# Attention with a sink and a window, then an MLP: where the sink scores of two pairs of chunks are computed

## The chip, the cores and the metric

The kernel runs on one core of a Trainium2 chip. The metric is the device time of one execution in microseconds. A second number is the span: the time from the first to the last instruction in the profile of one execution. TensorE (PE) does the matrix products, VectorE (DVE) and ScalarE (ACT) the work on elements, GpSimd (POOL) small work and the issue of loads, SyncE (SP) the issue of stores and of transposes by DMA.

## The reference

Attention for 4 batches, 8 heads, 768 positions of 64 elements; a query sees the first 4 positions (the sink) and the 128 positions up to its own. The result is reshaped to rows of 512, normalised, put through a two-layer MLP and added to itself.

```python
scores = scale * np.matmul(q, k.transpose(0, 1, 3, 2))
is_sink = pos[None, :] < int(n_sink)               # n_sink = 4
rel = pos[:, None] - pos[None, :]
in_window = (rel >= 0) & (rel < int(window))       # window = 128
scores = np.where(is_sink | in_window, scores, -1000000000.0)
a = softmax(scores);  x = (a @ v) as rows of 512   # shortened
xn = (x - mu) / np.sqrt(var + 1e-06) * g_ln
out = x + np.maximum(xn @ w_ch1, 0.0) @ w_ch2
```

## The kernel before

The 3072 rows are 24 tiles of 128 rows (index t), two to a chunk (index c, 0 to 11), three chunks to a batch. So chunks 3, 6 and 9 begin a batch, chunks 5, 8 and 11 end one.

Every operation is written down once with `P.op(name, engines and costs, priority, emit, reads, writes, ...)`. `Plan.run` (line 114) then plays the program through with the costs, picks on each engine the ready operation of the lowest priority number, and gives out buffers from rings. The order it arrives at is emitted. So what a change of a priority or of a cost does to the order is seen only in the order itself. Rings that matter here: `nat` (8 buffers, line 415) for queries and keys as loaded, `kT` (4) and `qT` (3, line 419) for the transposed ones, `ps` (3, line 421) for the sink weights, and the PSUM banks `one` (4) and `pair` (2).

From chunk 4 on, `chunk(c)` (line 654) issues for k and q two loads each on POOL (line 704; 128 KB each, four to a chunk), and on SP two transposes by DMA for each (`DMA_TRANSPOSE`, issued in `dma_t`, line 578). The loads wait for `gate(c)`: the small step `rs` (lines 891 and 892, on POOL) of an earlier tile. The transposes of q also wait for the transpose of a normalised tile (`trx`, also line 578, xnt<-xc in the profile), which the matrix stage L1047 of that chunk reads. Loads of v follow (`load_m`, line 632).

From chunk 3 on, `block(t)` (line 916) is one visit of TensorE for a tile. It has four parts in this order: the products of the tile before with v (L954, L961, L970), the scores of tile t inside the window (L981, `pair` banks, pieces of 64 by 64), and in a chunk's first visit the sink scores of both its tiles (L989): eight matmuls that give 32 rows each to a strip of the output and are 128 columns wide (64 in a batch's first chunk). ACT makes exponentials of the scores (L999) and of the sink scores (L1009, into `ps`). Between the visits run the MLP's products: `mlp(c)` (line 1029) with L1047 (the first layer, reads xnt) and L1075 (the second).

The last loop (from line 1093 on) calls `chunk(c)` and `block` in order of c.

Of the kernel before, what the change touches and what calls it, by code (L numbers as in the profile page):

```python
# [9 lines left out]
AF = mybir.ActivationFunctionType  # L10
# [215 lines left out]

LOW, HIGH = 1e-9, 1e9
LAST_CUTS, LAST_ACT = (0, 320, 512), (3,)
NEG = -1e30
NEVER = -1e9  # L230
BIG = 3.3e38
# [138 lines left out]
def kernel(  # L370
# [203 lines left out]
    def gate(c):  # L574
        return [rs_op[2 * c - (4 if c > 5 else 5)]] if PAR["by_dma"] < c < NC else []
# [78 lines left out]
    def chunk(c):  # L654
        b, R = c // RC, c % RC
        d = at(c, "tr") if c >= 2 else early(2 * c)
        ld = d - 14.0 if c >= RC else 4.0
        if c < 2:
            kT_b[c], qT_b[c] = Buf(f"kT{c}", "kT"), Buf(f"qT{c}", "qT")
            if c == 0:  # L660
                nats = [Buf("kf", "natf"), Buf("qf", "natf")]
                for hh in range(2):
                    hs = slice(4 * hh, 4 * hh + 4)
                    for i, (x, T) in enumerate(((k, kT_b[c]), (q, qT_b[c]))):
                        nm, src, part = "kq"[i], nats[i], Buf(f"{'kq'[i]}l{hh}")
                        ap = x[b, hs, 0:256, :].rearrange("h (p i) d -> p h (i d)", i=2)
                        P.op(f"{nm}ld{hh}", {("SP" if i == 0 else "ACT"): (0.53, 0.53)}, -70 + hh,
                             lambda e, src=src, ap=ap, hs=hs: (nc.sync if e == "SP" else nc.scalar).dma_start(
                                 src.t[:, hs].rearrange("p h i d -> p h (i d)"), ap), writes=[src, part], dma=HW_F)
                        nat, pt, done = Buf(f"{nm}c{hh}", "natc"), Buf(f"pt{nm}{hh}", "one"), Buf(f"{nm}T0{hh}")  # L670
                        P.op(f"cast{nm}{hh}", {"DVE": dve(512), "ACT": act(512)}, d + 0.01 * hh,
                             lambda e, nat=nat, src=src, hs=hs: (nc.scalar.copy if e == "ACT" else V.tensor_copy)(
                                 nat.t, src.t[:, hs].rearrange("p h i d -> p i h d")),
                             reads=[part], hold=[src], writes=[nat])

                        def tr(e, pt=pt, nat=nat):
                            pb = pt.t.rearrange("p (h i m) -> p h i m", h=2, i=2)
                            for hp in range(2):
                                for i in range(2):
                                    nc.tensor.matmul(pb[:, hp, i, :], lhsT=nat.t[:, i, 2 * hp:2 * hp + 2, :], rhs=ident,  # L680
                                                     start=hp + i == 0, stop=True, skip_group_check=True)
                        o = P.op(f"tr{nm}{hh}", pe(0.23), d + 0.02 + 0.01 * hh, tr, reads=[nat, Bc["ident"]], hold=[T], writes=[pt])
                        trs[0], trs[1] = trs.get(0, [o]), [o]
                        evict(f"ev{nm}0{hh}", d + 0.05 + 0.01 * hh, 512,
                              lambda pt=pt: pt.t.rearrange("p (h i m) -> p h m i", h=2, i=2),
                              lambda T=T, hh=hh: T.t[:, 2 * hh:2 * hh + 2, :].rearrange("p h (m i) -> p h m i", i=2), [pt], [T, done], fp=True)
                        for t in range(2):
                            tile_of[nm, t, hh] = done
            else:
                for i, (x, T) in enumerate(((k, kT_b[c]), (q, qT_b[c]))):  # L690
                    by_pairs(c, [("kq"[i], x, T, PAR["ld1"] + 0.01 * i)], d + 0.01 * i)
        else:
            both = []
            for nm, src, bT in (("k", k, kT_b), ("q", q, qT_b)):
                T = Buf(f"{nm}T{c}", nm + "T")
                bT[c] = T
                if c < PAR["by_dma"]:
                    both.append((nm, src, T, ld + (0.1 if nm == "q" else 0.0)))
                    continue
                for i in range(2):  # L700
                    nat = Buf(f"{nm}n{c}{i}", "nat")
                    ap = src[b, :, 256 * R + 128 * i:256 * R + 128 * (i + 1), :].rearrange("h p d -> p h d")
                    P.op(f"{nm}ld{c}{i}", {"POOL": (0.87, 0.9)}, ld + 0.01 * i + (0.1 if nm == "q" else 0.0),
                         lambda e, nat=nat, ap=ap: G.dma_start(nat.t, ap), writes=[nat], dma=SW, after=gate(c))  # L704
# [211 lines left out]
    def block(t):  # L916
# [4 lines left out]
        if t < NT:  # L921
# [11 lines left out]
            reads += [kT, qT] + ([kprev] if r and not i else []) + ([kts_b[b]] if sinks else [])  # L933
            writes += pps + ([pp_s] if sinks else [])
            hold += pes + ([held["ps", c]] if sinks else [])
# [14 lines left out]
        def go(e):  # L950
# [24 lines left out]
            for hp in range(HP):  # L975
                u, col = hp // 2, 192 * (hp % 2)
                for g, kt, k0, c0, q0, n in ((u, kT, own, 0, own, 128), *([(1 - u, kprev, old + 64, 0, own, 128)] if r else []),
                                             *([(u, kprev, old, 128, own, 64)] if r else []), (1 - u, kT, own + 64, 128, own + 64, 64)):
                    for h2 in range(2):
# [1 line left out]
                        nc.tensor.matmul(pps[u].t[64 * g:64 * g + 64, h2, col + c0:col + c0 + n],  # L981
                                         lhsT=kt.t[rs, hp, k0:k0 + 64], rhs=qT.t[rs, hp, q0:q0 + n],
                                         start=col == 0 and c0 == (128 if g != u and not r else 0), stop=True, skip_group_check=True)
            if sinks:
                for hp in range(HP):
                    for qh in range(2):
                        u = hp // 2
                        p0 = 64 * (qh ^ u) + 32 * (hp % 2)
                        nc.tensor.matmul(pp_s.t[p0:p0 + 32, 128 * u + 64 * (not r):128 * u + 128], lhsT=kts_b[b].t[:, hp, :],  # L989
                                         rhs=qT.t[:, hp, :].rearrange("p (i u c) -> p u i c", i=2, u=2)[:, qh, 0 if r else 1:2],  # L990
                                         start=True, stop=True, skip_group_check=True)
        cost = (0.0 if t == NT else 0.33 if r else 0.22) + (0.0 if not last else (0.36 if lr else 0.24) + (0.12 if lr else 0.06) + (0.115 if last["ps"] else 0.0))
        end = t < NT and sinks
        P.op(f"sc{t}", pe(cost + ((0.2 if r else 0.15) if end else 0)), d, go, reads=reads, writes=writes, hold=hold, mode=(("n" if lr else "r") if last else "q", "c" if end else "q"))
        if t < NT:
            scores.setdefault(c, P.ops[-1])
            for j in range(n_pair):
# [9 lines left out]
            if sinks:  # L1007
                lo = 0 if r else 64
                P.op(f"sx{c}", {"ACT": act(256 - 2 * lo)}, d + 0.3, lambda e: nc.scalar.activation(  # L1009
                    held["ps", c].t.rearrange("p (u c) -> p u c", u=2)[:, :, lo:128],  # L1010
                    pp_s.t[:, 0:256].rearrange("p (u c) -> p u c", u=2)[:, :, lo:128], AF.Exp, scale=scale),
                     reads=[pp_s], writes=[held["ps", c]])
        if last:
            st, x, xc = last["made"]
            x_b[t - 1], xst_b[t - 1] = x, st
# [191 lines left out]
```

## Time and profile before

| what | value |
| --- | --- |
| median of 3 runs | 215.82 us (215.72 to 217.69) |
| the profiled execution's own time | 215.85 us |
| its span | 214.3 us |
| L1047 and L1075 on TensorE | 86.5 and 84.3 us busy |
| L989 on TensorE, all sink scores | 72 matmuls; 48 of 128 columns, 24 of 64 |
| the first and the last of them start | 47.7 and 174.3 us |
| queue of POOL's loads (q0) | 13.18 MB |
| queue of SP's and ACT's transfers (q1) | 13.71 MB |

PE is the engine's matmuls, PEld its weight loads, SPq the DMA instructions that SP issues. A row of a timeline has the start and the length in microseconds (from the first start to the last end of the merged instructions), the engine, the line, the operation, output<-input, the tile in rows*columns, the shape, and the count. "(idle before <-releaser)" is in brackets where the engine stood idle. A few per cent of the matmul records are missing from a trace.

### The profile page before, as it was taken

The numbers are of one execution on the slowest core, as the hardware profiler recorded it, in microseconds if no ns is written. First come the engines' busy times: TensorE is split into PE (matmuls) and PEld (weight loads), VectorE is DVE, ScalarE is ACT, GpSimd is POOL, SyncE is SP. The second block draws the span as 40 slices with busy tenths as digits, with TensorE's granted clock in tenths as the row PEclk, the third lists the DMA queues.
The fourth block names the chain that finished last, engine by engine and source line by source line (L and its number), as shares of the span: only waits on it lengthen the run. The fifth ranks groups of instructions, "written<-read, shape, count | busy, mean of one in ns | idle before, by whom it ended". The sixth has DMA issues, their size and how long they took to land.

```text
span 214.3 us, 6540 instructions
## 1 busy us (share of the span) xinstructions
PE 205.8 (96%) x2682; PEld 143.4 (67%) x2704; DVE 114.3 (53%) x316; ACT 110.2 (51%) x179; POOL 112.4 (52%) x167
## 2 busy tenths in 40 slices
PE   7799999999999999999999999999999999999994
PEld 2567874755865865864865865864865865865853
DVE  4688884798355356356355456446355445444021
ACT  3797488195652562562562562562562562530610
POOL 7978732499971980970970980971971201202000
PEclk9999999999999999999999999999999999999999
DMA  5999999999999999899799999799899302202103
GB/s 152 189 189 206 193 208 192 177 162 161 159 192 152 135 139 125 129 132 175 105 147 133 98 145 161 120 129 162 111 137 137 98 3 73 77 0 74 52 0 107
DMA packets 104586, 28.04 MB, mean 131 GB/s; under 512 B 94820, under 2 KB 101608, under 8 KB 104552
## 3 DMA queue, kind: packets, MB, share of 16 engines
q0 software_dynamic: 69904, 13.18, 86.1%
q1 hardware_dynamic: 33448, 13.71, 35.8%
q10 hardware_dynamic: 1200, 0.69, 1.1%
q8 instruction: 22, 0.36, 0.8%
q14 instruction: 12, 0.10, 0.2%
HBM read 27.43 MB, written 6.29 MB: 157 GB/s over the span
## 4 chain that ended last, share of the span: by engine, by line
PE 92%; DMA 3%; DVE 1%; issue 1%; ACT 1%; ACTq 0%; DVEq 0%
PE one L1047 39%; PE one L1075 39%; PE pair L981 3%; DMA natf<-in_q_dram 3%; PE one L954 2%; PE one L961 2%; PE one L970 1%; PE one L989 1%; PE pair L731 1%; PE one L859 1%; PE one L899 1%; PE pair L606 1%; PE one L599 1%; PE pair L752 0%; PE pair L859 0%
## 5 line engine op out<-in xcount | busy, mean ns | idle before, releaser
L1075 PE MATMUL one<-w,h 128*128 128x512 bf16 (+2 forms) x378 | 84.3, 370 | 2.2 <-issue 1.6
L1047 PE MATMUL one<-xnt,w 128*128 128x256 bf16 x768 | 86.5, 273 | 0.0
L1047 PEld LDWEIGHTS <-w 128*128 128x128 bf16 x768 | 74.8, 98 | 11.2 <-issue 0.4
L1057 ACT ACTIVATE h<-one 128x512 bf16<-128x512 f32 x95 | 56.7, 597 | 47.3 <-PE one L1047 47.3
L1075 PEld LDWEIGHTS <-h 128*128 128x128 bf16 x400 | 37.1, 98 | 40.1
L999 ACT ACTIVATE pe<-pair 128x768 bf16<-128x768 f32 x36 | 27.2, 809 | 41.0 <-PE pair L981 41.0
L891 POOL TENSOR_SCALAR st<-st 128x1 f32<-128x1 f32 x24 | 9.0, 373 | 66.7 <-DVE st L884 66.2
L646 POOL DMA_DIRECT2D vn<-in_v_dram x59 | 38.7, 704 | 9.2 <-DMA w<-in_moe_w_ch_dram 6.7
L1022 DVE RECIPROCAL rec<-one 128x4 f32<-128x4 f32 x36 | 6.4, 178 | 63.0 <-PE one L970 51.5
L1084 DVE SCALAR_TENSOR_TENSOR ot<-one,st,x 128x512 f32<-128x512 f32 (+2 forms) x25 | 18.2, 727 | 20.3 <-PE one L1075 14.2
L892 POOL TENSOR_TENSOR st<-st,mhalf 128x1 f32<-128x1 f32 x24 | 16.8, 701 | 2.0
L882 DVE BATCH_NORM_STATS2 st<-x 128x6 f32<-128x512 bf16 x24 | 16.7, 695 | 0.8
L1024 DVE TENSOR_TENSOR x<-one,rec 128x256 bf16<-128x256 f32 x36 | 15.3, 425 | 1.2
L704 POOL DMA_DIRECT2D nat<-in_k_dram x16 | 15.1, 944 | 0.0
L704 POOL DMA_DIRECT2D nat<-in_q_dram x16 | 14.2, 904 | 0.0
L1004 DVE TENSOR_TENSOR pe<-pe,band 128x768 bf16<-128x768 bf16 x24 | 12.2, 551 | 0.0
L981 PE MATMUL pair<-qT,kT 64*64 64x128 bf16 (+1 forms) x528 | 9.2, 204 | 0.0
L886 DVE TENSOR_SCALAR xc<-x,st 128x512 bf16<-128x512 bf16 x24 | 8.5, 353 | 0.9
L954 PEld LDWEIGHTS <-pe 128*128 128x128 bf16 (+1 forms) x144 | 6.2, 97 | 2.9 <-issue 0.8
L779 ACT ACTIVATE pe<-pair 128x1024 bf16<-128x1024 f32 (+1 forms) x8 | 7.1, 916 | 1.5 <-PE pair L731 1.2
L981 PEld LDWEIGHTS <-kT 64*64 64x64 bf16 x528 | 7.2, 108 | 0.4 <-ACT w L1111 0.4
L954 PE MATMUL one<-vn,pe 128*128 128x65 bf16 (+1 forms) x144 | 7.0, 193 | 0.0
(111 smaller groups left out, 151.0 us busy)
## 6 DMA issues: line engine op xcount, KB each, us to landing
out_dram<-ot SPq DMA_DIRECT2D x23, 256.0 KB
w<-in_moe_w_ch_dram POOLq DMA_DIRECT2D x8, 512.0 KB, 12.4
nat<-in_k_dram POOLq DMA_DIRECT2D x16, 128.0 KB, 5.2
nat<-in_q_dram POOLq DMA_DIRECT2D x16, 128.0 KB, 5.9
vn<-in_v_dram POOLq DMA_DIRECT2D x44, 32.0 KB, 6.1
vn<-in_v_dram POOLq DMA_DIRECT2D x15, 64.0 KB, 6.0
natp<-in_k_dram POOLq DMA_DIRECT2D x3, 256.0 KB, 14.3
vn<-in_v_dram POOLq DMA_DIRECT2D x6, 128.0 KB
```

The costliest lines, as they stand in the source:

```text
L646: P.op(f"vld{t}_{i}", {"POOL": (0.8, 0.85)}, prio + 0.001 * i, lambda e, p0=p0, n=n, hs=hs, src=src: G.dma_start(m.t[p0:p0 + n, hs, 0:64], ...
L704: lambda e, nat=nat, ap=ap: G.dma_start(nat.t, ap), writes=[nat], dma=SW, after=gate(c))
L882: P.op(f"bn{t}", {"DVE": fix(0.60)}, d + 0.12, lambda e: V.bn_stats(st.t[:, 8:14], x.t), reads=[x], writes=[st, mv])
L892: G.tensor_tensor(st.t[:, 16:17], st.t[:, 17:18], mhalf, op=ALU.pow)),
L954: nc.tensor.matmul(po[h // 4].t[:, 65 * (h % 4):65 * (h % 4) + 65], lhsT=pe_[rs, col:col + 128], rhs=vn_b[t - 1].t[rs, h, :], start=h % 4 ...
L981: nc.tensor.matmul(pps[u].t[64 * g:64 * g + 64, h2, col + c0:col + c0 + n], lhsT=kt.t[rs, hp, k0:k0 + 64], rhs=qT.t[rs, hp, q0:q0 + n], st ...
L999: nc.scalar.activation(pes[j].t.rearrange("p a b -> p (a b)")[:, 0:768].rearrange("p (a b) -> p a b", a=2), pps[j].t[:, :, 0:384], AF.Exp, ...
L1024: P.op(f"x{t - 1}{u}", {"DVE": dve(256)}, d + 0.051 + 0.002 * u, lambda e, u=u, rc=rc, pv=pv: V.tensor_tensor(x.t[:, 256 * u:256 * u + 256 ...
L1047: nc.tensor.matmul(ph.t[:, 256 * s:256 * s + 256], lhsT=w1[ht // 4][:, j, 128 * (ht % 4):128 * (ht % 4 + 1)], rhs=xnt.t[:, j, :], start=j ...
L1057: nc.scalar.activation(hb.t, ph.t, AF.Relu)
L1075: nc.tensor.matmul(pc.t[:, 0:wd], lhsT=(h1[2 * s + i].t[:, 128 * ii:128 * ii + 128] if by_tile else h1[ht // 2].t[:, 256 * (ht % 2) + 128 ...
L1084: V.scalar_tensor_tensor(ot.t[:, sl], in0=pc.t[:, 0:wd], scalar=st.t[:, 16:17], in1=x.t[:, sl], op0=ALU.mult, op1=ALU.add),
```

## The change

A table `SINKS_WITH = {7: 8, 10: 11}` names pairs of chunks. Chunk 8's sink scores are computed in chunk 7's first visit, chunk 11's in chunk 10's: sixteen sink matmuls there, in the two halves of one PSUM bank, and none in the first visits of chunks 8 and 11. Two operations on ACT follow, one for each chunk's `ps`. For that the queries of chunks 8 and 11 are needed a chunk earlier: their loads and transposes get priorities that are smaller by 16 (a chunk), and wait for an earlier `rs` and an earlier `trx`. Chunk 8's and 11's `chunk()` is written down right after that of 7 and 10, as `block` reads its `qT`. The number of instructions stays the same.

The order of the emitted program changes in these places: on POOL the two q loads of chunk 8 go from behind its k loads to right behind `rs` of tile 9, those of chunk 11 to right behind `rs` of tile 15. On SP the two q transposes of chunk 8 go to the place ahead of chunk 7's k transposes, those of chunk 11 ahead of chunk 10's. On ACT the two sink operations are neighbours. From chunk 8 on the `one` banks are given out in another rotation, and the `nat` and `qT` buffers in another order.

```diff
+SINKS_WITH = {7: 8, 10: 11}
...
+                    lead = nm == "q" and c in SINKS_WITH.values()
-                    P.op(f"{nm}ld{c}{i}", {"POOL": (0.87, 0.9)}, ld + 0.01 * i + (0.1 if nm == "q" else 0.0),
-                         lambda e, nat=nat, ap=ap: G.dma_start(nat.t, ap), writes=[nat], dma=SW, after=gate(c))
-                    P.op(f"tr{nm}{c}{i}", {"SP": (1.2, 1.2)}, d + 0.01 * i, lambda e, T=T, nat=nat, i=i: dma_t(
+                    P.op(f"{nm}ld{c}{i}", {"POOL": (0.87, 0.9)}, ld + 0.01 * i + (0.1 if nm == "q" else 0.0) - (16.0 if lead else 0.0),
+                         lambda e, nat=nat, ap=ap: G.dma_start(nat.t, ap), writes=[nat], dma=SW, after=[rs_op[2 * c - 7]] if lead else gate(c))
+                    P.op(f"tr{nm}{c}{i}", {"SP": (1.2, 1.2)}, d + 0.01 * i - (16.0 if lead else 0.0), lambda e, T=T, nat=nat, i=i: dma_t(
                         T.t[:, :, 128 * i:128 * i + 128], nat.t.rearrange("p h d -> p (h d)")),
-                        reads=[nat], writes=[T], dma=HW_X, after=[trx_op[2 * c - 3]] if c > PAR["by_dma"] and nm == "q" else [])
+                        reads=[nat], writes=[T], dma=HW_X, after=[trx_op[2 * c - (6 if lead else 3)]] if c > PAR["by_dma"] and nm == "q" else [])
...
-            sinks = i == 0
-            if sinks:
-                held["ps", c] = Buf(f"ps{c}", "ps")
+            sinks = [] if i or c in SINKS_WITH.values() else [c, SINKS_WITH[c]] if c in SINKS_WITH else [c]
+            for sc_ in sinks:
+                held["ps", sc_] = Buf(f"ps{sc_}", "ps")
...
-            if sinks:
+            for n, sc_ in enumerate(sinks):
                 for hp in range(HP):
                     for qh in range(2):
-                        u = hp // 2
+                        u, full = hp // 2, r or n
                         p0 = 64 * (qh ^ u) + 32 * (hp % 2)
-                        nc.tensor.matmul(pp_s.t[p0:p0 + 32, 128 * u + 64 * (not r):128 * u + 128], lhsT=kts_b[b].t[:, hp, :],
-                                         rhs=qT.t[:, hp, :].rearrange("p (i u c) -> p u i c", i=2, u=2)[:, qh, 0 if r else 1:2],
+                        nc.tensor.matmul(pp_s.t[p0:p0 + 32, 256 * n + 128 * u + 64 * (not full):256 * n + 128 * u + 128], lhsT=kts_b[b].t[:, hp, :],
+                                         rhs=qT_b[sc_].t[:, hp, :].rearrange("p (i u c) -> p u i c", i=2, u=2)[:, qh, 0 if full else 1:2],
                                          start=True, stop=True, skip_group_check=True)
...
-        P.op(f"sc{t}", pe(cost + ((0.2 if r else 0.15) if end else 0)), d, go, reads=reads, writes=writes, hold=hold, mode=(("n" if lr else "r") if last else "q", "c" if end else "q"))
+        P.op(f"sc{t}", pe(cost + (((0.09 if r else 0.04) + 0.11 * len(sinks)) if end else 0)), d, go, reads=reads, writes=writes, hold=hold, mode=(("n" if lr else "r") if last else "q", "c" if end else "q"))
...
-                P.op(f"sx{c}", {"ACT": act(256 - 2 * lo)}, d + 0.3, lambda e: nc.scalar.activation(
+                P.op(f"sx{sc_}", {"ACT": act(256 - 2 * lo)}, d + 0.3 + n, lambda e, n=n, sc_=sc_, lo=lo: nc.scalar.activation(
...
     for c in range(NC):
-        chunk(c)
+        if c not in SINKS_WITH.values():
+            chunk(c)
+        if c in SINKS_WITH:
+            chunk(SINKS_WITH[c])
```

More of the change, by code (lines that the diff above doesn't have):

```diff
@@ L932, in block @@
             held[t] = dict(ps=ps, made=made, pes=pes)
-            reads += [kT, qT] + ([kprev] if r and not i else []) + ([kts_b[b]] if sinks else [])
+            reads += [kT, qT] + ([kprev] if r and not i else []) + ([kts_b[b]] if sinks else []) + [qT_b[sc_] for sc_ in sinks[1:]]
             writes += pps + ([pp_s] if sinks else [])
-            hold += pes + ([held["ps", c]] if sinks else [])
+            hold += pes + [held["ps", sc_] for sc_ in sinks]
         if last:
@@ L983, in go @@
                                          start=col == 0 and c0 == (128 if g != u and not r else 0), stop=True, skip_group_check=True)
-            if sinks:
+            for n, sc_ in enumerate(sinks):
                 for hp in range(HP):
                     for qh in range(2):
-                        u = hp // 2
+                        u, full = hp // 2, r or n
                         p0 = 64 * (qh ^ u) + 32 * (hp % 2)
-                        nc.tensor.matmul(pp_s.t[p0:p0 + 32, 128 * u + 64 * (not r):128 * u + 128], lhsT=kts_b[b].t[:, hp, :],
-                                         rhs=qT.t[:, hp, :].rearrange("p (i u c) -> p u i c", i=2, u=2)[:, qh, 0 if r else 1:2],
+                        nc.tensor.matmul(pp_s.t[p0:p0 + 32, 256 * n + 128 * u + 64 * (not full):256 * n + 128 * u + 128], lhsT=kts_b[b].t[:, hp, :],
+                                         rhs=qT_b[sc_].t[:, hp, :].rearrange("p (i u c) -> p u i c", i=2, u=2)[:, qh, 0 if full else 1:2],
                                          start=True, stop=True, skip_group_check=True)
         cost = (0.0 if t == NT else 0.33 if r else 0.22) + (0.0 if not last else (0.36 if lr else 0.24) + (0.12 if lr else 0.06) + (0.115 if last["ps"] else 0.0))
-        end = t < NT and sinks
-        P.op(f"sc{t}", pe(cost + ((0.2 if r else 0.15) if end else 0)), d, go, reads=reads, writes=writes, hold=hold, mode=(("n" if lr else "r") if last else "q", "c" if end else "q"))
+        end = t < NT and bool(sinks)
+        P.op(f"sc{t}", pe(cost + (((0.09 if r else 0.04) + 0.11 * len(sinks)) if end else 0)), d, go, reads=reads, writes=writes, hold=hold, mode=(("n" if lr else "r") if last else "q", "c" if end else "q"))
         if t < NT:
@@ L1006, in block @@
                 P.op(f"mk{t}_{j}", {"DVE": dve(768, 0.52)}, d + 0.2 + 0.05 * j, mk, reads=[Bc["band"]], rw=[pes[j]])
[L1007 to L1012, printed above, removed]
+            for n, sc_ in enumerate(sinks):
+                lo = 0 if r or n else 64
+                P.op(f"sx{sc_}", {"ACT": act(256 - 2 * lo)}, d + 0.3 + n, lambda e, n=n, sc_=sc_, lo=lo: nc.scalar.activation(
+                    held["ps", sc_].t.rearrange("p (u c) -> p u c", u=2)[:, :, lo:128],
+                    pp_s.t[:, 256 * n:256 * n + 256].rearrange("p (u c) -> p u c", u=2)[:, :, lo:128], AF.Exp, scale=scale),
+                     reads=[pp_s], writes=[held["ps", sc_]])
         if last:
```

## The prediction

> **What bounds the kernel now.** I read the page first: its span, the busy shares and the chain that ended last.
>
> ```profile
> span 214.3 us, 6540 instructions
> PE 205.8 (96%) x2682; PEld 143.4 (67%) x2704; DVE 114.3 (53%) x316; ACT 110.2 (51%) x179; POOL 112.4 (52%) x167
> PE 92%; DMA 3%; DVE 1%; issue 1%; ACT 1%; ACTq 0%; DVEq 0%
> ```
>
> TensorE is busy for 96% of the span and is 92% of the chain. No other engine passes 53%. So only what TensorE does, or waits for, moves the end. The next view is the table of stretches, cut at the places where the change moves transfers.
>
> ```profile
> 82.00:89.00 7.00, 6.84 (x103) 5.12 (x103) 4.68 (x14) 3.23 (x5) 3.01 (x5) 1.00 0.47 106
> 89.00:98.00 9.00, 8.95 (x106) 6.14 (x106) 3.87 (x10) 4.74 (x9) 6.76 (x10) 1.00 2.01 137
> 131.00:137.00 6.00, 5.84 (x97) 4.49 (x97) 3.95 (x10) 2.85 (x5) 2.63 (x4) 1.00 0.73 119
> ```
>
> Columns: stretch and length, then busy time of PE, weight loads, DVE, ACT and POOL, the granted clock, the DMA share, GB/s. TensorE has at most 0.16 us of idle time in a stretch, at a clock of 1.00. The DMA share swings between 2.01 while a chunk's K, Q and V come in (89 to 98) and 0.47 or 0.73 between two chunks. Those calm stretches are where the change puts its early loads.
>
> Then the timeline of TensorE over chunk 8's two visits, the first with sink scores (L989), the second without.
>
> ```profile
> 125.38 0.52 PE L981 MATMUL pair<-qT,kT 64*64 64x128 bf16 x32
> 125.83 0.30 PE L989 MATMUL one<-qT,kts 128*32 128x128 bf16 x8
> 126.06 5.35 PE L1075 MATMUL one<-w,h 128*128 128x512 bf16 x23
> 131.85 0.52 PE L981 MATMUL pair<-qT,kT 64*64 64x128 bf16 x32
> 132.53 1.67 PE L1075 MATMUL one<-w,h 128*128 128x512 bf16 x7 [0.16 <-issue]
> ```
>
> Read literally, the sinks cost nothing: from the first L981 to the first L1075 it is 0.68 us both times. But the code issues 24 and 8 matmuls of L1075 here, and the rows show 23 and 7: records are missing. The weight loads are complete, so I take the weight loads' timeline instead.
>
> ```profile
> 125.35 0.41 PEld L981 LDWEIGHTS <-kT 64*64 64x64 bf16 x32
> 125.83 0.12 PEld L989 LDWEIGHTS <-kts 128*32 128x32 bf16 x8
> 126.05 4.86 PEld L1075 LDWEIGHTS <-h 128*128 128x128 bf16 x24
> 131.82 0.41 PEld L981 LDWEIGHTS <-kT 64*64 64x64 bf16 x32
> 132.30 1.41 PEld L1075 LDWEIGHTS <-h 128*128 128x128 bf16 x8
> ```
>
> With sinks 126.05 - 125.35 = 0.70 us, without 132.30 - 131.82 = 0.48 us. The "0.16 <-issue" in front of L1075 is the place of the missing first matmul, not a wait. **One sink visit costs 0.22 us of TensorE.**
>
> **The change part by part.** *Removed:* the sink visits of chunks 8 and 11, 2 x 0.22 = 0.44 us, all on the path.
>
> *Added:* eight more sink matmuls in the visits of chunks 7 and 10. The trace has no visit with sixteen, so I bound them with a visit whose eight have half the columns.
>
> ```profile
> 93.52 0.24 PE L989 MATMUL one<-qT,kts 128*32 128x64 bf16 x8
> 93.70 5.35 PE L1075 MATMUL one<-w,h 128*128 128x512 bf16 x23
> ```
>
> From the first L989 to L1075 it is 93.70 - 93.52 = 0.18 us for 64 columns and 126.06 - 125.83 = 0.23 us for 128. So 64 columns more cost 0.05, and eight matmuls of 128 columns stream for 0.10: the lower end. The upper end is the whole 0.23, if the second eight pay all that the first eight pay. In between lies what the eight do among themselves: the outputs use four column strips, so they run as two rounds of four, and a timeline that starts inside the visit shows the second round.
>
> ```profile
> 125.90 0.22 PE L989 MATMUL one<-qT,kts 128*32 128x128 bf16 x2
> ```
>
> It starts 125.90 - 125.83 = 0.07 us after the first. Two more rounds are 0.14 us, and I take that, as the second chunk's rounds follow in the same tiling. Added: 2 x 0.14 = 0.28 us, between 0.20 and 0.46. More matmuls in the same stream can't be a gain.
>
> Here a rule of the Trainium skill speaks against the change. The page "TensorE: Matmul & The Clock Gate", section "The mechanism", says that a weight load overlaps a running matmul only when its row group differs (it also names a background weight buffer as a way out). All sink loads use all 128 rows, so by the rule none of the added ones would overlap. The rows disagree: eight loads take 0.12 us together. What it would give is among the rivals.
>
> *ACT.* The exponential of the later chunk's sinks moves to the earlier visit.
>
> ```profile
> 109.63 1.51 ACT L999 ACTIVATE pe<-pair 128x768 bf16<-128x768 f32 x2 [0.30 <-PE pair L981]
> 111.03 0.39 ACT L1009 ACTIVATE ps<-one 128x256 bf16<-128x256 f32 x1
> 116.10 1.51 ACT L999 ACTIVATE pe<-pair 128x768 bf16<-128x768 f32 x2 [4.68 <-PE pair L981]
> ```
>
> ACT is then idle for 4.68 us, so 0.39 us more is hidden, and the result is needed only a chunk later. The "one" bank stays taken 0.39 us longer; its next user comes with the next visit, some 5 us later. Without this cover the cost would be 0.39 us each. Cost: none.
>
> *POOL.* Two loads of queries (128 KB each) move ahead of the next rs step and the k loads.
>
> ```profile
> 79.97 0.72 POOL L892 TENSOR_TENSOR st<-st,mhalf 128x1 f32<-128x1 f32 x1
> 85.91 0.38 POOL L891 TENSOR_SCALAR st<-st 128x1 f32<-128x1 f32 x1 [5.21 <-DVE st L884]
> 87.06 1.87 POOL L704 DMA_DIRECT2D nat<-in_k_dram  x2
> 134.28 0.38 POOL L891 TENSOR_SCALAR st<-st 128x1 f32<-128x1 f32 x1 [5.21 <-DVE st L884]
> ```
>
> They issue in the idle 5.21 us before 85.91, and before 134.28 for the second pair, and take about 1.8 us, so nothing behind them is late. If they did wait past that, the rs step, and with it the output sums that use it, would be late. They take two of the eight nat buffers each time, last read by the transposes of chunk 5's keys and chunk 7's queries, long done. Later on POOL, chunk 8's loads lose two entries; nothing on TensorE waits for them. Cost and gain: none.
>
> *SP.* This is the step with a risk: two DMA transposes of queries now stand ahead of the k transposes of chunks 7 and 10, and behind those stands the transpose of xnt that the matrix stage of chunks 5 and 8 (L1047) reads.
>
> ```profile
> 84.23 2.59 SPq L578 DMA_TRANSPOSE qT<-nat  x2
> 88.23 0.53 SPq L1088 DMA_DIRECT2D out_dram<-ot  x1
> 92.00 3.45 SPq L578 DMA_TRANSPOSE kT<-nat  x2
> 96.08 1.19 SPq L578 DMA_TRANSPOSE xnt<-xc  x1
> 98.63 3.74 SPq L578 DMA_TRANSPOSE qT<-nat  x2
> ...
> 136.21 0.34 SPq L1088 DMA_DIRECT2D out_dram<-ot  x1
> 139.69 3.59 SPq L578 DMA_TRANSPOSE kT<-nat  x2
> 144.46 1.19 SPq L578 DMA_TRANSPOSE xnt<-xc  x1
> ```
>
> ```profile
> nat<-in_q_dram POOLq DMA_DIRECT2D x16, 128.0 KB, 5.9
> ```
>
> A query load lands 5.9 us after issue: issued at about 80.7 and 81.6, both are there by 87.5; SP gets to them at 88.76. Then SP is idle until 92.00, as the keys have not landed: 3.24 us. The pair takes 2.59 us, at its longest here 3.74: 88.76 + 3.74 = 92.50, the k pair to 95.95, and xnt still issues at 96.08, when its input is ready. At the second place 136.55 + 3.74 + 3.59 = 143.88, before 144.46. Hidden, with 0.13 and 0.58 us left in the worst case. The qT buffers they take were last read by the visits of chunks 4 and 7, which are done by then. Chunk 7's own q pair (98.63) moves on by no more than 1 us, and its visit is at 109.
>
> *The new wait on TensorE.* The visits of chunks 7 and 10 now also wait for chunk 8's and 11's queries, and all of TensorE's work is queued behind them. The queries are transposed from 88.76 on, chunk 7's first L989 is at 109.6 by the ACT row above (109.63): some 17 us of margin, and as much at chunk 10. Cost: none.
>
> *Sum:* -0.44 + 0.28 = -0.16 us (between -0.24 and +0.02). The profiled execution took 215.85 us, of which the span is 214.3; the median of the runs is 215.82, so it stands for them. Predicted: 215.85 - 0.16 = **215.7 us**.
>
> **The rivals.**
>
> *A, slower: the matrix stage waits for xnt.* The early transposes share the DMA engines with the loads of chunk 7's keys (share 2.01 from 89 on), and the keys land late. If the loads lose the whole 2.59 us, the k pair ends at 92.00 + 2.59 + 3.45 = 98.04 and xnt issues 1.96 us late; at the second place 139.69 + 2.59 + 3.59 = 145.87, 1.41 us late.
>
> ```profile
> 101.55 1.69 PE L1047 MATMUL one<-xnt,w 128*128 128x256 bf16 x14
> ```
>
> L1047 starts at 101.55 behind L1075 without a wait, 5.47 us after xnt was issued; how much of that is slack, no row shows. With none, 3.4 us are lost: 219.1. With half of it as slack, 217.4. It decides from the point where xnt is issued more than that slack after 96.08. Against it: the pair falls into the ramp of the loads, which POOL issues from 87.06 on at 0.9 us each, and the share just before is 0.47. The page "DMA: Bandwidth & Descriptors", section "Queues, rings and completion order", says that an engine takes turns between its queues packet by packet; by that rule the loads would give up a part of the engines, not wait for the whole pair. Chance 0.12, of which 0.05 lies over 218.0.
>
> *B, the removed visit gives nothing back,* because the change of tiling before L1075 costs what the sinks did (the literal 0.68 = 0.68). Then only the added 0.28 stays: 216.1. The complete weight loads speak against it. Chance 0.08.
>
> *C, the added loads run one after another.* Eight loads and eight matmuls in single file at 0.12 / 8 + 0.07 each would be 0.68 us per pair instead of 0.14, so 215.69 + 1.08 = 216.8. The two rounds seen (0.07 apart, four at a time) speak against it. Chance 0.04. This is where the rule on row groups leads.
>
> *D, much faster,* as chunk 8's and 11's transfers get relief: TensorE has no such waits to give back (5.84 of 6.00, 8.95 of 9.00 busy). Chance 0.01 or 0.02.
>
> **How the numbers follow.** The forecast, 215.4 to 216.0, has 0.74. Adding B and C and the smaller part of A gives the range 215.2 to 216.9, also because the three runs shown spread from 215.72 to 217.69. A measurement of this kernel can tell about 1% (2.2 us) from no change; the forecast, B and C are all within it. Faster by over 1%: 0.02. Within: 0.91. Slower: 0.07 (the upper part of A, and what I have not thought of).
>
> **What would show it.** Right: L989 in seven visits instead of nine, two of them with sixteen matmuls; in those, 0.14 us more from L981 to L1075, and 0.48 instead of 0.70 between the weight loads in the visits of chunks 8 and 11; ACT with two L1009 in a row near 111; SP with a q pair at 88.8, and xnt still at about 96.1. Wrong: idle time in front of L1047 near 101.5 or 150 (A), or in front of the visits of chunks 7 and 10 (late queries), or 0.2 us or more for the added eight (B, C).

## The result, and the profile after

The changed kernel takes 217.24 us in the median (216.22 to 219.98, 22 runs), the kernel before 215.77 us (215.62 to 217.69, 22 runs): ratio 1.0065, interval 1.0053 to 1.0077. So it is 1.4 us slower, and the forecast was 0.16 us faster, with a range from 215.2 to 216.9. (The 219.98 is one execution in a slower state of the chip; the ratio leaves it out.) The profiled execution took 217.09 us. (L1047, L1075, L981, L989 are L1049, L1077, L983, L991 after the change.)

The page of the changed kernel:

```profile
span 215.6 us, 6534 instructions
...
PE 206.8 (96%) x2682; PEld 143.7 (67%) x2704; DVE 114.4 (53%) x316; ACT 110.1 (51%) x179; POOL 111.9 (52%) x167
...
PE 75%; DMA 14%; DVE 4%; issue 3%; POOL 2%; ACT 1%; SPq 0%; POOLq 0%; DVEq 0%
...
L1049 PE MATMUL one<-xnt,w 128*128 128x256 bf16 x768 | 86.5, 273 | 1.0 <-DMA xnt<-xc 0.9
```

The busy shares look the same as before. The chain does not: TensorE had 92% of it and DMA 3%, now 75% and 14%. The first layer of the MLP (L1049) is as busy as before (86.5) but now has 1.0 us of idle time ahead of it, nearly all ended by xnt. The waits of the changed kernel (engine, what, releaser: total us, times, longest):

```profile
POOL vn L647 <- DMA nat<-in_k_dram: 4.2, 2, 2.2
...
PEld L1049 <- DMA xnt<-xc: 1.9, 2, 1.0
...
PE one L1049 <- DMA xnt<-xc: 0.9, 2, 0.5
```

Two waits for xnt, one at each place; the kernel before has none at this line. (POOL's two are waits for the key loads; no wait of TensorE is for the values that they hold up.) To size the two waits I take the distance from the start of L1075's last seven matmuls to the start of L1047. First the kernel before, first and second place (101.55, the first place's L1047, stands in the prediction):

```profile
100.04 1.67 PE L1075 MATMUL one<-w,h 128*128 128x512 bf16 x7 [0.16 <-issue]
...
148.42 1.67 PE L1075 MATMUL one<-w,h 128*128 128x512 bf16 x7 [0.16 <-issue]
149.93 3.33 PE L1047 MATMUL one<-xnt,w 128*128 128x256 bf16 x29
```

It is 1.51 us at both. Then the kernel after:

```profile
100.40 1.67 PE L1077 MATMUL one<-w,h 128*128 128x512 bf16 x7 [0.16 <-issue]
102.40 1.81 PE L1049 MATMUL one<-xnt,w 128*128 128x256 bf16 x15 [0.33 <-DMA xnt<-xc]
...
149.17 1.67 PE L1077 MATMUL one<-w,h 128*128 128x512 bf16 x7 [0.16 <-issue]
151.38 1.81 PE L1049 MATMUL one<-xnt,w 128*128 128x256 bf16 x15 [0.54 <-DMA xnt<-xc]
```

2.00 and 2.21 us: the waits are **0.49 and 0.70 us**, 1.19 together. The queue of SP in the kernel after:

```profile
89.27 2.72 SPq L579 DMA_TRANSPOSE qT<-nat  x2
92.10 5.16 SPq L579 DMA_TRANSPOSE kT<-nat  x2
97.35 1.22 SPq L579 DMA_TRANSPOSE xnt<-xc  x1
...
137.41 2.64 SPq L579 DMA_TRANSPOSE qT<-nat  x2
140.76 5.51 SPq L579 DMA_TRANSPOSE kT<-nat  x2
146.36 1.22 SPq L579 DMA_TRANSPOSE xnt<-xc  x1
```

The early pair takes 2.72 and 2.64 us, as predicted. But the k pair behind it now takes 5.16 and 5.51 us (before 3.45 and 3.59), and xnt is issued at 97.35 and 146.36 (before 96.08 and 144.46). The reason for the longer k pair is in the trace's records of finished DMAs: chunk 7's second key load lands at 96.05, before it was 93.83, and at the second place at 145.06, before 142.03.

The weight loads of chunk 7's first visit (sixteen sinks) and chunk 8's first visit (none):

```profile
109.97 0.41 PEld L983 LDWEIGHTS <-kT 64*64 64x64 bf16 x32
110.45 0.23 PEld L991 LDWEIGHTS <-kts 128*32 128x32 bf16 x16
110.78 4.86 PEld L1077 LDWEIGHTS <-h 128*128 128x128 bf16 x24
...
126.32 0.41 PEld L983 LDWEIGHTS <-kT 64*64 64x64 bf16 x32
126.80 4.86 PEld L1077 LDWEIGHTS <-h 128*128 128x128 bf16 x24
```

110.78 - 109.97 = 0.81 us against 0.70 before: eight more sinks cost 0.11 us. 126.80 - 126.32 = 0.48, as predicted: 0.22 us saved. The visits of chunks 10 and 11 give the same two numbers. So the tensor part is 2 x 0.11 - 2 x 0.22 = -0.22 us. With the waits, 1.19 - 0.22 = +0.97 us. The span grew by 1.3; the other 0.36 stands already at 100.40 against 100.04, ahead of the first wait. It is there at 77 us too (a visit's weight loads start at 77.33 against 76.97), before the first moved load is issued (81.02), so it is no part of the change but a difference between two executions.

Last, the busy share of the DMA engines between 86 and 104 us, in forty slices of 0.45 us (9 is 90% or more), before and after:

```profile
DMA  2192192499999999999999529999999972960006
```

```profile
DMA  9993291699999999999199999999999999999999
```

And the stretches in which the waits lie, before and after (last two columns: DMA share, GB/s). The share adds up the times of all packets that start in the stretch, over 16 engines; it passes 1 where their times overlap.

```profile
98.00:104.00 6.00, 5.84 (x83) 3.99 (x83) 4.12 (x11) 2.62 (x4) 2.13 (x4) 1.00 0.78 140
...
147.00:153.00 6.00, 5.84 (x86) 4.27 (x86) 3.95 (x10) 2.96 (x5) 2.75 (x4) 1.00 0.66 122
```

```profile
98.00:104.00 6.00, 5.51 (x77) 3.30 (x77) 4.43 (x11) 2.03 (x3) 1.85 (x4) 1.00 1.98 174
...
147.00:153.00 6.00, 5.30 (x76) 3.20 (x76) 4.24 (x11) 2.05 (x3) 2.00 (x3) 1.00 2.02 150
```

Before, the slices empty from about 101 us and are at 0 by 102.2; after, they show 9 to the end. The share of 98 to 104 goes from 0.78 to 1.98, the rate only from 140 to 174 GB/s.

### The profile page after: what moved, and what is told of

It reads as the page before. It is cut to its first block, busy times and chain, and to the rows that moved or that the text cites. A ratio compares the mean times of both kernels' runs of the same rounds, so it can differ in the third digit from the quotient of the medians.

```text
span 215.6 us, 6534 instructions
## 1 busy us (share of the span) xinstructions
PE 206.8 (96%) x2682; PEld 143.7 (67%) x2704; DVE 114.4 (53%) x316; ACT 110.1 (51%) x179; POOL 111.9 (52%) x167
## 4 chain that ended last, share of the span: by engine, by line
PE 75%; DMA 14%; DVE 4%; issue 3%; POOL 2%; ACT 1%; SPq 0%; POOLq 0%; DVEq 0%
PE one L1049 33%; PE one L1077 30%; DMA nat<-in_k_dram 7%; DMA xnt<-xc 5%; DMA natf<-in_k_dram 2%; PE pair L983 2%; PE one L956 2%; PE one L963 1%; DVE st L884 1%; PE one L972 1%; DVE x L1026 1%; PE pair L733 1%; PE one L861 1%; PE one L901 1%; POOL st L893 1%
## 5 line engine op out<-in xcount | busy, mean ns | idle before, releaser
L1049 PE MATMUL one<-xnt,w 128*128 128x256 bf16 x768 | 86.5, 273 | 1.0 <-DMA xnt<-xc 0.9
L1077 PE MATMUL one<-w,h 128*128 128x512 bf16 (+2 forms) x378 | 84.3, 370 | 2.2 <-issue 1.4
L1049 PEld LDWEIGHTS <-w 128*128 128x128 bf16 x768 | 74.6, 98 | 12.7 <-DMA xnt<-xc 1.9
L1077 PEld LDWEIGHTS <-h 128*128 128x128 bf16 x400 | 37.1, 98 | 40.0
L893 POOL TENSOR_SCALAR st<-st 128x1 f32<-128x1 f32 x24 | 8.4, 349 | 62.9 <-DVE st L886 62.4
L983 PE MATMUL pair<-qT,kT 64*64 64x128 bf16 (+1 forms) x528 | 9.2, 204 | 0.0
L983 PEld LDWEIGHTS <-kT 64*64 64x64 bf16 x528 | 7.2, 108 | 0.4 <-ACT w L1116 0.4
```

The costliest lines, as they stand in the source:

```text
L1049: nc.tensor.matmul(ph.t[:, 256 * s:256 * s + 256], lhsT=w1[ht // 4][:, j, 128 * (ht % 4):128 * (ht % 4 + 1)], rhs=xnt.t[:, j, :], start=j ...
L1077: nc.tensor.matmul(pc.t[:, 0:wd], lhsT=(h1[2 * s + i].t[:, 128 * ii:128 * ii + 128] if by_tile else h1[ht // 2].t[:, 256 * (ht % 2) + 128 ...
```

## The experiments

Two theories came in turn. **T**: the early transposes make the key loads late, so xnt is issued late by SP's order. **U**, formed after the run with one pair of chunks: when xnt is issued is not the point; all that was put on the DMA engines ahead of it has to drain first, and the two early transposes add 2.3 us to that, while TensorE had 1.5 us to spare. All ratios are against the kernel before, run on the same chip. A landing is that of the one execution that was profiled for each kernel. Code is cut where "..." stands.

### Only the moves

The loads and transposes move as in the change; the sinks stay where they were.

```diff
-            sinks = [] if i or c in SINKS_WITH.values() else [c, SINKS_WITH[c]] if c in SINKS_WITH else [c]
+            sinks = [] if i else [c]
```

> Only the early loads and transposes of the queries of chunks 8 and 11; each chunk's sink scores stay in its own visit, so TensorE does the work of the kernel before. Theory T (the early transposes, standing ahead of the keys on SP and sharing the DMA engines with the key loads, make xnt late for L1047): all of the loss and none of the gain, 1.007 to 1.009 of before, with waits in front of L1047 near 102 and 151 us. Rival S (the sixteen sink matmuls in one visit cost the time): no change, 1.000.

217.28 us, ratio 1.0077 (1.0051 to 1.0103). L1049 waits in both places:

```profile
102.28 1.92 PE L1049 MATMUL one<-xnt,w 128*128 128x256 bf16 x16 [0.70 <-DMA xnt<-xc]
...
151.06 2.14 PE L1049 MATMUL one<-xnt,w 128*128 128x256 bf16 x18 [0.23 <-DMA xnt<-xc]
```

So the loss is all in the moves, none of it in TensorE's new work. In this execution the second key load was not late (it landed at 92.98); xnt was issued 0.59 us later than before all the same (96.67), and landed at 102.23 instead of 100.06.

### Only the sinks

Sixteen sinks in the visits of chunks 7 and 10, none in those of 8 and 11, with SP and POOL in the order of before. The later chunk's sink scores are computed from the earlier chunk's queries, so that no query has to come early.

```diff
-                    lead = nm == "q" and c in SINKS_WITH.values()
+                    lead = False
...
-                                         rhs=qT_b[sc_].t[:, hp, :]...
+                                         rhs=qT.t[:, hp, :]...
```

> Only the sink part: sixteen sink matmuls in the visits of chunks 7 and 10, none in those of 8 and 11, with no transfer moved; the later chunk's sink scores are computed from the earlier chunk's queries, so that part of the output is not the reference's. Theory T: the pure gain of TensorE, 0.22 us less than before, 0.999. Rival S: slower than before by most of the loss, 1.004 or more.

215.61 us (215.41 to 215.87), ratio 0.9994 (0.9985 to 1.0003); the median is 0.13 us under the kernel before (215.74). It agrees with the forecast's -0.16 in size, though the interval doesn't exclude nothing.

### The early transposes later, or xnt first

Two ways to get xnt out of the way. In the first, chunk 8's q transposes stand behind chunk 7's (`trx_op[2 * c - 5]` for `- 6`, and 15.9 for 16.0). In the second they stay where they are, and chunk 7's k transposes wait for xnt:

```diff
-                        ... if c > PAR["by_dma"] and nm == "q" else [])
+                        ... if c > PAR["by_dma"] and (nm == "q" or c in SINKS_WITH) else [])
```

> The change with the early loads kept, but the early transposes of chunk 8's and 11's queries put behind those of chunk 7's and 10's queries on SP, in the calm stretch from about 101 us on. Theory T: no wait in front of L1047, xnt issued at 96.1, the gain of TensorE stays: 0.999 of before. Rival L (the early loads on POOL are what delays the keys): as slow as the change, 1.006.

> The change with the early transposes where they are, but the transposes of the keys of chunks 7 and 10 put behind xnt on SP, so that late keys no longer hold xnt. If the place on SP's queue is what makes xnt late (T, order): xnt is issued at 96.1, no wait in front of L1047, 0.999 of before. If the data in flight on the DMA engines alone make xnt land late (T, engines): xnt is issued in time but still lands late, 1.003 or more.

The first: 216.29 us, ratio 1.0022 (0.9999 to 1.0045), where 0.999 was expected. No wait for xnt, but no gain either. SP had put one of the two transposes behind the next xnt, and it landed at 109.26 for sink matmuls at 109.66. The profiled execution (215.69 us) shows no wait there; a margin of 0.4 us may be used up in others, but none of those was profiled.

The second: 216.67 us, ratio 1.0031 (1.0014 to 1.0048). Its waits and its SP queue:

```profile
PE one L991 <- DMA qT<-nat: 1.2, 2, 0.9
```

```profile
102.67 2.10 SPq L579 DMA_TRANSPOSE xnt<-xc  x1
104.88 1.23 SPq L579 DMA_TRANSPOSE qT<-nat  x1
```

The wait for xnt is gone, and another has taken its place: chunk 7's own second q transpose is issued at 104.88 (in the kernel before both were issued by 102.37), and the sinks of chunk 7 wait for it. xnt is issued in time (96.19) and still lands at 101.09, 1.03 us later than before, though the k transposes no longer stand ahead of it. The second of the two expectations has the late landing, but not the time: the only new wait of the profile is that for qT, so the ratio of 1.0031 says nothing on xnt.

### All four q transposes behind xnt and ahead of the next

As the first of the two above, and the xnt of tile 12 (18) waits for the early pair.

```diff
+                    if lead:
+                        x_op = trx_op[2 * c - 4]
+                        x_op.deps.append(P.ops[-1])
...
```

> Theory T (the two early q transposes cost time only because they run beside the loads of chunk 7's and 10's keys and stand on SP ahead of the xnt transpose of the matrix stage): here all four q transposes of a pair of chunks stand together, behind the xnt of the stage of chunks 5 and 8 and ahead of the next one (tiles 12 and 18). No wait for xnt at L1049, none for qT at L991, and the gain of the tensor part (0.15 to 0.2 us) comes out: 215.55, ratio 0.999, faster than the run with the transposes later but one of them behind xnt (1.0022). Rival: two more transposes anywhere in the run cost their share of the DMA engines: ratio at or above 1.003, with a wait for xnt of tile 12 or 18 in the rows, which is now issued some 4 us later than before.

215.59 us, ratio 0.9999 (0.9986 to 1.0013), the median 0.17 us under the 215.76 of the kernel before. No wait for xnt or qT:

```profile
96.03 1.19 SPq L579 DMA_TRANSPOSE xnt<-xc  x1
98.15 0.33 SPq L1095 DMA_DIRECT2D out_dram<-ot  x1
98.59 5.82 SPq L579 DMA_TRANSPOSE qT<-nat  x4
```

The same transposes cost nothing here, and the query loads are as early as in the change. So neither the loads on POOL nor "two more transposes" are the cause, but the place. The tensor part's gain of 0.15 to 0.2 us may be in it, but the interval includes no change.

### Earlier still

The early pair stands one place further ahead, before xnt of tile 10.

```diff
-    after=[trx_op[2 * c - (6 if lead else 3)]] ...
+    after=[] if lead else [trx_op[2 * c - 3]] ...
+                    if lead:
+                        x_op = trx_op[2 * c - 6]
+                        x_op.deps.append(P.ops[-1])
...
```

> The early q transposes stand one place earlier on SP, ahead of the output store and the xnt of tile 10 (about 2.4 us before their place in the change, before the data of chunk 7's keys begin to move). Theory T: less overlap with the key loads, so the second key load lands less than 1 us later than before instead of 2.2, the k pair takes under 4.3 us, and the ratio is 1.003 or less. Rival (a place on SP ahead of the xnt is enough, whatever the loads do): as slow as the change, 1.0065, with the same two waits at L1049.

216.44 us (5 runs), ratio 1.0033 (1.002 to 1.0046): about half the loss. The second key load lands at 93.14 and the k pair takes 4.03 us, as T had expected. In the profiled one, the fastest of the five (215.69 us), xnt lands at 101.50 for a stage that begins at 101.65; 0.15 us is all that is left of the 1.49. T and U both allow this.

### Plain copies in place of the transposes

The early transposes become plain copies of the same 128 KB; the queries of chunks 8 and 11 are then not transposed, so this part of the output is not the reference's.

```diff
-  lambda e, ...: dma_t(T.t[...], nat.t.rearrange("p h d -> p (h d)"))
+  lambda e, ...: (nc.sync.dma_start if lead else dma_t)(T.t[...], nat.t.rearrange("p (a b) d -> p a (b d)", a=HP) if lead else ...)
```

> The two early transposes of each pair are replaced by plain copies of the same 128 KB at the same place on SP; the queries of chunks 8 and 11 are then not transposed, so that part of the output is not the reference's. If it is the bytes and the turns of the queues that delay the key loads: second key load 2 us late, waits at L1049 of 0.5 and 0.7, ratio 1.006 as the change. If it is the way a transpose goes through the DMA engines (many small elements): k pair at 3.5 to 4 us as before, no wait at L1049, ratio 0.999.

216.32 us (215.73 to 217.25), ratio 1.0019 (1.0001 to 1.0038): between the two. The profiled one is near the slowest (217.21 us):

```profile
89.38 1.41 SPq L708 DMA_DIRECT2D qT<-nat  x2
91.84 4.33 SPq L580 DMA_TRANSPOSE kT<-nat  x2
96.26 1.31 SPq L580 DMA_TRANSPOSE xnt<-xc  x1
```

xnt is issued almost in time (96.26), and lands at 103.07; L1050, as the first layer's line is called in this run, starts at 103.11. So copies can delay xnt as much as transposes, at least in one execution. That the median is lower leaves open whether a transpose takes more of the engines than a copy; neither of the two expectations was met.

### One pair of chunks only

```diff
-SINKS_WITH = {7: 8, 10: 11}
+SINKS_WITH = {7: 8}
```

> Only chunks 7 and 8 are paired; chunks 10 and 11 are as before. If the two waits for xnt are independent: one wait at L1049 of about 0.5 us, none at the second place, a gain of 0.1 from the tensor part, so +0.4 to +0.6 us, ratio about 1.002 to 1.003. If the loss has another source that any early pair sets off (a shift of all that follows): over 1.004; if the two places together are needed: 1.000.

216.71 us, ratio 1.0055 (1.0034 to 1.0075), more than the half that I expected; 1.002 to 1.003 is missed. Its profile is what T can't explain:

```profile
92.24 3.53 SPq L579 DMA_TRANSPOSE kT<-nat  x2
96.09 1.22 SPq L579 DMA_TRANSPOSE xnt<-xc  x1
```

```profile
102.50 1.70 PE L1049 MATMUL one<-xnt,w 128*128 128x256 bf16 x14 [0.78 <-DMA xnt<-xc]
```

Here the k pair takes 3.53 us and xnt is issued at 96.09, as in the kernel before (96.08). The keys were not late: the second load landed at 93.73. Yet xnt lands at 102.46 instead of 100.06, and TensorE waits 102.50 - 100.05 - 1.51 = 0.94 us (100.05 is the start of L1077's last seven matmuls). **An xnt that is issued on time lands 2.4 us late**, behind the loads and transposes that were put on the engines before it. From this came U.

### The values later

The change as it is, and the 256 KB of values of chunks 7 and 10 go behind xnt. The control has the same edit in the kernel before.

```diff
-    after=list(ones_of.values()) + gate(t // 2))
+    after=list(ones_of.values()) + ([rs_op[2 * (t // 2) - 3]] if t // 2 in SINKS_WITH else gate(t // 2)))
```

> The change as it is, but the six loads of values of chunks 7 and 10 (256 KB each time) wait on POOL for the rs step of tile 11 (17), so they are issued at about 98 instead of 91, behind the xnt transpose. Theory U (all that is put on the DMA engines ahead of xnt has to drain before xnt lands; the early transposes add 2.3 us to that, the slack is 1.6): the values no longer stand ahead, xnt lands at 100.5 or earlier though the two early transposes stay where they are, no wait for xnt at L1049, ratio 0.999 to 1.001. Theory T (what counts is the key loads being late and SP's order): the keys land late all the same, xnt issues at about 97 and its wait stays, ratio 1.005 or more.

> Control: the kernel before with nothing but the later loads of values of chunks 7 and 10. Theory U: xnt was in time anyway, so ratio 0.999 to 1.001; if the later values make a wait of their own it shows here, over 1.002.

215.49 us, ratio 0.9987 (0.9972 to 1.0003); the control 215.80 us, 1.001 (0.9997 to 1.0023). The three rows of the first from POOL's, SP's and TensorE's timelines:

```profile
96.79 4.08 POOL L647 DMA_DIRECT2D vn<-in_v_dram  x6
```

```profile
95.96 1.19 SPq L579 DMA_TRANSPOSE xnt<-xc  x1
```

```profile
101.42 2.78 PE L1049 MATMUL one<-xnt,w 128*128 128x256 bf16 x24
```

The early transposes are where the change has them (89.14 us), and the wait is gone: xnt lands at 99.24, with less ahead of it. T's 1.005 is out by a wide margin. At this place the keys were not late (93.35). At the second place they were: the second key load landed at 144.20 (before 142.03) and xnt was issued at 145.50, 1.04 us later than before. It landed at 148.99 all the same, 0.70 us ahead of TensorE, so late keys alone do not make the wait. The gain does not come from the later values as such, since the control has none. This version is the lowest median of all, 0.27 us under the kernel before; its interval includes no change.

### Half the dose, and twice

Of the early pair only the first transpose stays early, and the second goes behind chunk 7's q transposes and ahead of the next xnt; or each is issued twice.

```diff
-    after=[trx_op[2 * c - (6 if lead else 3)]] ...
+    after=[trx_op[2 * c - ((5 if i else 6) if lead else 3)]] ...
...
```

```diff
+                    for n in range(2 if lead else 1):
+                        P.op(f"tr{nm}{c}{i}{n}", ...
```

> Half the dose: of the two early q transposes of a pair only the first stays ahead of the k transposes, the second goes behind the q transposes of chunk 7 (10) and ahead of the next xnt. Theory U: xnt lands 1.1 to 1.2 us later than before, within the slack of 1.6, so no or hardly a wait for xnt, ratio 0.999 to 1.002. If any transpose ahead of the keys is enough: 1.004 or more.

> Twice the dose: each of the early q transposes is issued twice in a row into the same place, so four stand ahead of xnt instead of two. Theory U: the slack is used up by the first two, so the second two cost nearly their whole 2.3 us at both places: waits for xnt of 2.5 to 3 us each, +4 to +6 us over before, ratio 1.019 to 1.028. If the transposes share the engines with other work without pushing it back: below 1.012.

Half: 215.60 us, ratio 0.9998 (0.9979 to 1.0018), no wait. xnt lands at 100.73, between the two cases and 0.84 us ahead of TensorE. That is 0.67 us later than before, less than the 1.1 to 1.2 that U gave.

Twice: 237.71 us, ratio 1.1012 (1.0981 to 1.1044), +22 us where U gave 4 to 6. It is not the doubled dose that I meant (L1050 is the first layer here too):

```profile
89.09 8.52 SPq L579 DMA_TRANSPOSE qT<-nat  x2
97.71 2.51 SPq L579 DMA_TRANSPOSE kT<-nat  x2
100.33 4.42 SPq L579 DMA_TRANSPOSE qT<-nat  x2
104.84 1.22 SPq L579 DMA_TRANSPOSE xnt<-xc  x1
```

```profile
110.42 9.66 PE L1050 MATMUL one<-xnt,w 128*128 128x256 bf16 x64 [8.79 <-DMA xnt<-xc]
```

The repeat writes the same place, and the program makes it wait until the first has landed: the profile has four such waits of SP for qT, the longest 6.0 us. Two transposes take 8.52 us, and all of SP's queue stands behind them. xnt is issued 8.8 us late and TensorE waits 8.79. The run tells nothing about bytes, but much about a wait at the head of SP's queue.

### What the runs say together

The first place in each profile but that of "twice". "Landed" is the last completion of the xnt DMA in the trace; "could start" is the start of L1075's last seven matmuls plus 1.51.

| kernel | q transposes ahead of xnt | xnt issued | landed | TensorE could start | did start |
| --- | --- | --- | --- | --- | --- |
| before | 0 | 96.08 | 100.06 | 101.55 | 101.55 |
| only the sinks | 0 | 96.06 | 99.65 | 101.53 | 101.53 |
| all four behind xnt | 0 | 96.03 | 98.84 | 101.50 | 101.50 |
| transposes later | 0 | 96.15 | 100.65 | 101.62 | 101.62 |
| the kernel before, values later | 0 | 95.92 | 98.32 | 101.39 | 101.39 |
| half the dose | 1 | 96.15 | 100.73 | 101.57 | 101.57 |
| one pair of chunks | 2 | 96.09 | 102.46 | 101.56 | 102.50 |
| only the moves | 2 | 96.67 | 102.23 | 101.41 | 102.28 |
| the change | 2 | 97.35 | 102.35 | 101.91 | 102.40 |
| the change, values later | 2 | 95.96 | 99.24 | 101.42 | 101.42 |
| earlier still | 2 | 96.19 | 101.50 | 101.65 | 101.65 |
| xnt first (no k transposes ahead) | 2 | 96.19 | 101.09 | 101.66 | 101.66 |
| plain copies | 2 copies | 96.26 | 103.07 | 101.63 | 103.11 |

With two ahead where the change puts them, xnt lands at 102.2 to 102.5 whether it is issued at 96.1 or at 97.35. With none it lands at 98.8 to 100.7 when the values are not moved. So single landings of one kind spread by almost 2 us, and the run with half the dose (100.73) can't be told from none. Take 256 KB of values out from ahead of the two transposes, and xnt is back at 99.2. In every row in which the values keep their place, xnt lands 0.2 to 0.6 us after the last of the values, which come on POOL's queue (before: 99.51 and 100.06; one pair: 102.11 and 102.46). That the engines drain what both queues gave them fits all of this. How they share the work is not shown.

## Why the prediction was wrong

- *What bounds the kernel:* right. TensorE's waits are all that moved the end.
- *Removed, 2 x 0.22:* right (0.70 to 0.48 us). *Added, 2 x 0.14:* 2 x 0.11. The reading by rounds was close (in the trace the added rounds start 0.056 us apart, against 0.07 in the sum); the row-group rule against the change (rival C) and rival B fell. "Only the sinks" confirms the direction.
- *ACT and POOL:* right at the price of nothing. The version with all four transposes behind xnt has the same early loads and the same exponentials, and loses nothing.
- *The wait for early queries:* right; no run shows a wait for them. The one wait for qT ("xnt first", 0.85 us) was for chunk 7's own queries.
- *SP, "Hidden, with 0.13 and 0.58 us left in the worst case", the cost none:* **this step failed.** It added up how long SP takes to issue (2.59 to 3.74 us a pair) and stopped where xnt is issued. Two things were wrong. The worst case was not the worst: the k pair took 5.16 and 5.51 us, as its second load was late. And an issue time is no landing time: with xnt issued at 96.09 it still landed 2.4 us late. What had to be added up is what the engines have to move between 89 and 101, and what had to be compared with it is TensorE's spare time at L1047, 1.49 us, which the prediction left unknown ("no row shows"). In the trace's records of finished DMAs it is 101.55 - 100.06 (at the second place 149.93 - 148.22 = 1.71). The missing term is +1.2 in the profile; by the medians, "only the moves" costs 1.5 us.
- *Rival A* had the place (L1047), the event (a wait for xnt) and, with half its delay as slack, the time: 217.4 for a measured 217.24. It had 0.12. That the time fits is partly luck: half the delay as slack was a guess, and the 1.7 us of waits that it adds measured 1.19. Its mechanism was half of the truth: the keys are late in the change, but not with one pair nor with only the moves, and xnt lands late in all three. The argument that held it down was that the pair falls into a ramp, with a share of 0.47 just before. But the pair was issued at 89.27, into the very stretch whose share is 2.01, and 0.47 was a mean over a stretch that ends there. The other argument was the Trainium skill, page "DMA: Bandwidth & Descriptors", section "Queues, rings and completion order": an engine takes turns between its queues packet by packet. No run here isolates the turns: behind the same two transposes the second key load landed 2.2 us later than before in the change, and 0.1 us earlier with one pair. The fault was to take the rule for comfort. If engines take turns, all that is queued lands later together, xnt at the end included.

## What to carry to other kernels

Here a transfer that was moved ahead of others delayed one that came behind it by over 2 us, without delaying its issue; and it was transfers of another queue, taken out from ahead, that made up for it. So cost a moved transfer by the landing of the last one that something waits for, not by the time at which its queue has issued it. Before a transfer is put into a stretch, read the DMA share at the moment of its issue, not the mean of the stretch before (here the share was 2.01, with a 9 in nearly every slice). Then the next wait's spare time is the budget (here 1.5 us, against 2.4 for two transposes of 128 KB). Put it behind the transfer that the bounding engine reads next, or take something out from ahead: both made the loss vanish here.

## What the runs showed of the hardware that was not expected

- 128 KB moved from SBUF to SBUF by transpose delayed what came behind it by about 1.2 us beside the loads of keys, queries and values (half of 102.46 - 100.06, for two; the landings with none ahead spread by almost 2 us, so this is an estimate). With the values out of the way it was about 0.5 us (half of 99.24 - 98.32). The Trainium skill, page "DMA: Bandwidth & Descriptors", section "Latency and other measured facts", gives 261 GB/s for a transpose with a non-contiguous middle dimension, which would be an estimate of 0.5 us each. The two runs with later values are near that; the run with one pair shows over twice as much, in company.
- Sixteen sink matmuls in one visit cost 0.11 us more than eight, and the first eight cost 0.22 more than none. So half of a sink visit's price is not the matmuls' own; that it is the change of tiling is my reading, which no run isolates.
- In the run with each transpose issued twice, TensorE's granted clock fell during the wait of 8.79 us (0.53 in 105 to 110, 0.50 in 110 to 115, 1.00 again in 118 to 120):

```profile
110.00:120.00 10.00, 9.59 (x67) 7.55 (x68) 0.00 (x0) 4.18 (x7) 0.00 (x0) 0.72 0.86 106
```

The third figure from the end, 0.72, is the mean granted clock; 64 matmuls of L1050 took 9.66 us there, against 7.15 in a stage of the same run without a wait (8.84 behind the second long wait, of 8.78 us). After the waits of 0.5 and 0.7 us of the change the clock stays at 1.00 (the rows of 98 to 104 and 147 to 153). So here the short waits cost themselves, and the long ones 2.5 and 1.7 us more.
